# Loading q and k two tokens to a packet in an attention and mixture-of-experts kernel

## The chip, the cores and the metric

The kernel runs on one core of a Trainium2 chip. The metric is the time of one execution on the device in microseconds (us). Before the change it is 764.48 us, the median of three runs (762.65 to 764.74).

A core has five engines that work side by side, each on its own list of instructions in fixed order: TensorE (PE in the profile; its weight loads are a row of their own, PEld), VectorE (DVE), ScalarE (ACT), GpSimd (POOL) and SyncE (SP), which here only issues transfers. They meet at semaphores. Sixteen DMA engines move data between HBM and the on-chip memory SBUF. TensorE writes to a second memory, PSUM, from which VectorE and ScalarE take its results.

## The reference, cut to what matters

```
B, H, S, D = 8, 8, 576, 64                # q, k, v: [B, H, S, D] f32
# attention on tokens averaged four by four (144 of them), repeated four times
out_up    = repeat(softmax(mean4(q) @ mean4(k).T / 8) @ mean4(v), 4)
# attention of each token to the tokens at a distance below 4
out_local = softmax(where(|i - j| < 4, q @ k.T / 8, -1e9)) @ v
x = (out_up + out_local) as [4608 tokens, 512]
# each token goes to one of 8 experts
logits = x @ w_gate + modality_bias[modality_id]
e = argmax(logits); g = softmax(logits)[e]
out = g * (relu(x @ w1[e]) @ w2[e])       # w1: [8, 512, 1024], w2: [8, 1024, 512]
```

## The kernel before

**Units.** Attention goes in 32 units, four to a batch entry; a unit is two heads, one on partitions 0 to 63 and one on 64 to 127 of what TensorE makes. Two units share one load of q and k: `load_qk(b, half)` brings four heads of both into `qt` and `kt`, with 96 tokens on the partitions (token 96 j + p on partition p). `tp` (L253 to L259) transposes 96 tokens of both heads at once, three times into one PSUM tile; `qT` (ScalarE, L271) scales and copies that into 288 columns of `qT`, `kT_` (VectorE, L275) into 288 columns of `kT`. A unit has two such halves (i = 0, 1) for q and two for k. The local scores (`sc`, L304) are 96 small products a unit on a mask that `mk` (L295) puts into PSUM first; the averaged tokens are sums over `qT` and `kT` (`qd`, `d`, `kd`), their scores `scd` (L331). Local probabilities go through a 32x32 transpose (`lt`) and `Pw_` (L372) to `avl` (L408), the product with v; the averaged ones through `pdt` (L378) and `PdT` to `avd` (L393). `X` adds both.

v comes twice: `load_v` as overlapping windows of 32 tokens, 24 apart (`vw`, two buffers by batch entry, a packet of 256 B for each window row and head), and `load_vg` as eight tokens to a packet (`vg`, three buffers) for the averages that GpSimd makes (`vt`, `vd_`).

**Order.** All this is written out by hand. `PHASE` gives each step of a unit a time, in units, after the unit's start; `build` makes a list of (unit + phase, function) in `calls`, sorts it, and calls it in a manual schedule. An engine's instructions stand in that order. Loads are in the same list: `load_qk` of half h at unit time 2 h - 2.02, `load_vg` of unit n at n - 0.14, `load_v` of the next batch entry in four parts from 4 b + 3.65 on. The loads before the loop (both halves of q and k of batch entry 0, v, the gate weights, the modality ids and biases in `Consts.load`) are issued first. `Consts.biases` (L154) turns the modality ids with a product on TensorE (L160) into a table of biases for all tokens; it is called at time 3.05.

**Router.** After four units a batch entry's tokens are routed: logits (`lg`, `LT`, `lgt`, `L`), the argmax and counts on VectorE (`ch1`, `ch2`, 8.39 and 8.55 after the start of the entry's first unit), the place of each token (`pr`, `pl`), a scatter of token numbers by GpSimd (`st`) and the store of the rows (`xr`, `R`, `store`) to HBM.

**Early units.** The experts work in units of 256 tokens of one expert. Two of them (`KEARLY`) are made up from the first five batch entries, before attention ends: `Router.early` counts tokens (a product, L574), makes a table of units (`units_of`, `table`, `index`: some twenty small VectorE instructions) and leaves `eidx` and `eei`; then GpSimd gathers entries and rows (`entries`, `gather`), `Moe.xsplit` transposes the rows on TensorE and splits them into a high part (ScalarE, L777) and the rest (VectorE, L778), and `Moe.wload` and `wsplit` load weights and split them in the same way (L729, L730). `early` is one call at t, just after the last scatter of batch entry 4 (unit time 26.22); each `xsplit` and `wsplit` is one call too.

After attention, `compute` and `second` run the experts' products (L794, L841) for all units, fed by weights that SyncE loads and ScalarE and VectorE split; the late table is made by `Router.late` with the same helpers.

Of the kernel before, what the change touches and what calls it, by code (L numbers as in the profile page):

```python
# [24 lines left out]
NB = 6  # L25
# [39 lines left out]
}  # L65

# [106 lines left out]
class Attention:  # L173
# [23 lines left out]
    def load_qk(s, b, half):  # L197
        nc = s.nc

        qt = s.ld.tile([96, 2, 6, 2, D], F32, name="qt")  # L200
        kt = s.ld.tile([96, 2, 6, 2, D], F32, name="kt")
        for g in range(2) if (b, half) == (0, 0) else (slice(0, 2),):
            for t, src in ((qt, s.q), (kt, s.k)):
                for a in range(2):
                    h = src[b, 4 * half + 2 * a : 4 * half + 2 * a + 2]
                    if g in (0, 1):
                        nc.sync.dma_start(t[:, g, :, a], h[g].rearrange("(j p) d -> p j d", j=6))
                    else:
                        nc.sync.dma_start(t[:, :, :, a].rearrange("p g j d -> p (g j) d"),
                                          h.rearrange("g (j p) d -> p (g j) d", j=6))  # L210
        s.QK[2 * b + half] = (qt, kt)

    def load_v(s, b, part):
# [39 lines left out]
    def tp(s, n, nm, i):  # L253

        src = s.QK[n // 2]["qk".index(nm)]
        p = s.t["tp", nm, n, i] = s.ps.tile([128, 3, 96], F32, name="tp", tag="T", bufs=3)
        for j in range(3):
            s.nc.tensor.transpose(p[:, j, :], src[:, n % 2, 3 * i + j].rearrange("p a d -> p (a d)"),
                                  s.C.ident[:96, :96])  # L259
# [7 lines left out]
    def qT(s, n, i):  # L267
# [3 lines left out]
        s.nc.scalar.mul(s.t["qT", n][:, 288 * i : 288 * i + 288], p.rearrange("m j p -> m (j p)"), QS)  # L271

    def kT_(s, n, i):
        p = s.t.pop(("tp", "k", n, i))
        s.nc.vector.tensor_copy(s.kT[n % 2][:, PAD + 288 * i : PAD + 288 * i + 288], p.rearrange("m j p -> m (j p)"))  # L275
# [149 lines left out]
class Router:  # L425
# [145 lines left out]
    def counts(s, nm):  # L571
        nc = s.nc
        cp = s.ps.tile([128, NE], F32, name="cp", tag="A", bufs=2)
        nc.tensor.matmul(cp, s.C.ones, s.acc, start=True, stop=True)  # L574
        c = s.tp.tile([128, NE], F32, name=nm + "c")
        nc.vector.tensor_copy(c, cp)
        return c

    def units_of(s, c, add, n, nm):

        ni = s.tp.tile([128, NE], I32, name=nm + "ni")
        s.nc.vector.tensor_scalar(ni, c, float(add), None, op0=ALU.add)
        s.nc.vector.tensor_scalar(ni, ni, 8, None, op0=ALU.logical_shift_right)
        s.nc.vector.tensor_copy(n, ni)

    def table(s, n, base, U, nm, pool, tag):
# [6 lines left out]
        nc.vector.tensor_tensor(m, C.ltri[:, :N, :N], n.unsqueeze(1).broadcast_to([128, N, N]), op=ALU.mult)  # L593
        nc.vector.tensor_reduce(incl, m, op=ALU.add, axis=AX.X)
        excl = tp.tile([128, N], F32, name=nm + "excl")
        nc.vector.tensor_tensor(excl, incl, n, op=ALU.subtract)

        off = tp.tile([128, N], F32, name=nm + "off")
        nc.vector.scalar_tensor_tensor(off, excl, -float(UNIT), base, op0=ALU.mult, op1=ALU.add)
        sh = [128, U, N]  # L600
# [6 lines left out]
        nc.vector.tensor_tensor(oh, incl.unsqueeze(1).broadcast_to(sh), ub, op=ALU.is_gt)  # L607
        nc.vector.tensor_tensor(o2, excl.unsqueeze(1).broadcast_to(sh), ub, op=ALU.is_gt)
        nc.vector.tensor_tensor(oh, oh, o2, op=ALU.subtract)
        r = tp.tile([128, 2, U], F32, name=nm + "r")  # L610
        for i, qv in enumerate((off, C.e2[:, :N])):
            nc.vector.tensor_tensor(o2, oh, qv.unsqueeze(1).broadcast_to(sh), op=ALU.mult)
            nc.vector.tensor_reduce(r[:, i], o2, op=ALU.add, axis=AX.X)
        nc.vector.scalar_tensor_tensor(r[:, 0], C.uf[:, :U], float(UNIT), r[:, 0], op0=ALU.mult, op1=ALU.add)
        return r, incl, excl

    def index(s, r, U, nm, count=None):
# [5 lines left out]
                                op=ALU.add)  # L623
        ei = tp.tile([128, U + 1], I32, name=nm + "ei")
        nc.vector.tensor_copy(ei[:, :U], r[:, 1, :U])
        if count is not None:
            nc.vector.tensor_copy(ei[:, U : U + 1], count)
        return idx, ei

    def early(s, K):  # L630
# [6 lines left out]
        nc.vector.tensor_scalar(d, excl, -1.0, float(K), op0=ALU.mult, op1=ALU.add)  # L637
        nc.vector.tensor_scalar(d, d, 0.0, None, op0=ALU.max)
        nc.vector.tensor_tensor(d, d, n, op=ALU.min)
        return s.index(r, K, "e")  # L640

    def late(s, c, pool):
# [4 lines left out]
        s.units_of(c, UNIT // 2 - 1, n[:, :NE], "m")  # L647
        s.units_of(c, UNIT - 1, n[:, NE:], "mh")
# [5 lines left out]
        s.r, s.incl, _ = s.table(n, base, NUMAX, "m", pool, "o")  # L654
        return s.index(s.r, NFULL + 1, "m")

    def rest(s):
# [13 lines left out]
        return s.index(r, NLOOP, "r", cnt)  # L671


class Moe:
# [25 lines left out]
    def chunk(s, e, which, c):  # L700
        return s.wsplit(s.wload(e, which, c), which)
# [12 lines left out]
    def wsplit(s, raw, which):  # L714
        nc = s.nc
        i = s.cw % s.nw
        s.cw += 1
# [7 lines left out]
        with ExitStack() as order:  # L725
            if HOLD <= s.cw <= NHOLD and s.after:
                for x in s.after:
                    order.enter_context(s.tc.issue_after(x.ins))
            nc.scalar.copy(hi, raw)  # L729
            nc.vector.tensor_tensor(lo, raw, hi.bitcast(F32), op=ALU.subtract)  # L730
# [355 lines left out]
```

## Time and profile before

| | |
|---|---|
| median of three runs | 764.48 us |
| profiled execution: its time, its span | 764.05 us, 762.4 us |
| TensorE busy, of it in 380 to 762.4 us | 695.0 us, 373.47 us |
| VectorE, ScalarE, GpSimd busy | 472.6, 422.2, 321.7 us |
| DMA packets, of them under 512 B | 207335, 134941 |
| granted TensorE clock, mean | 0.95 |

The span runs from the first to the last instruction of the program; the rest of the execution's time lies around it. A busy row counts the union of an engine's instructions; TensorE's ends are modelled, so back-to-back products count as busy throughout. A wait is put down to whatever released the semaphore last; "issue" means that nothing in the profile released it. "L258" is a line of the kernel, "tp<-ident,qt" what is written and read, "96*128" rows and columns of the array that are used, "x3" that three like it follow each other. The attention units run from about 6 to 311 us, the experts' products from about 296 us to the end.

### The profile page before, as it was taken

Reading aid. Unit: us, or ns where it says so; the run is one execution under the profiler, and the core shown is the slowest. Engines: PE = TensorE matmul, PEld = TensorE weight load, DVE = VectorE, ACT = ScalarE, POOL = GpSimd, SP = SyncE. Lnnn points to the kernel's source line nnn. Section 1 sums busy time; section 2 is a strip of 40 time slices with the busy share of each in tenths; the row PEclk is TensorE's granted clock in tenths of the full one; section 3 lists DMA queues with packets and bytes.
Section 4 is the critical chain, followed back from the end, with each engine's and each line's share of the span. In section 5 each row is a group of like instructions: output and inputs, shape, how many; then the busy total and the mean of one; then the engine's idle time right before and its main releaser. Section 6 shows DMA issues by size and latency. Waiting matters only on the chain. (4 is left out here: it accounts for less than half of the span.)

```text
span 762.4 us, 20954 instructions
## 1 busy us (share of the span) xinstructions
PE 695.0 (91%) x8307; PEld 599.1 (79%) x8307; DVE 472.6 (62%) x956; ACT 422.2 (55%) x876; POOL 321.7 (42%) x369
## 2 busy tenths in 40 slices
PE   7499888999888978997899999999999999999995
PEld 4387666777666757885898899988999888999894
DVE  4377856778586867784765556555566555565620
ACT  2267756676655676754565545555546455465620
POOL 5365839486776867034433323223232242222101
PEclk8589998999997999998899999999999999999998
DMA  9999999989987982749797666766676766666500
GB/s 180 162 172 193 161 194 178 216 167 196 201 163 163 192 221 99 214 147 302 264 317 240 208 230 227 242 223 215 205 269 208 236 210 213 226 221 228 188 13 19
DMA packets 207335, 151.00 MB, mean 198 GB/s; under 512 B 134941, under 2 KB 173889, under 8 KB 207234
## 3 DMA queue, kind: packets, MB, share of 16 engines
q1 hardware_dynamic: 198978, 130.41, 68.4%
q0 software_dynamic: 8256, 19.22, 7.2%
q8 instruction: 67, 1.10, 0.7%
q14 instruction: 34, 0.28, 0.1%
HBM read 130.38 MB, written 19.47 MB: 197 GB/s over the span
## 5 line engine op out<-in xcount | busy, mean ns | idle before, releaser
L730 DVE TENSOR_TENSOR wlo<-raw,whi 128x1024 fp32r<-128x1024 f32 x130 | 159.3, 1235 | 135.8 <-ACT whi L729 134.9
L729 ACT CAST whi<-raw 128x1024 fp32r<-128x1024 f32 x130 | 135.5, 1048 | 126.7 <-PE l L794 60.2
L794 PE MATMUL l<-xh,wlo 128*128 128x256 f32 x488 | 139.1, 285 | 0.0
L794 PE MATMUL l<-xh,whi 128*128 128x256 f32 x488 | 138.3, 285 | 0.7 <-ACT xh L777 0.7
L794 PE MATMUL l<-xl,whi 128*128 128x256 f32 x488 | 138.7, 285 | 0.0
L845 POOL DMA_INDIRECT out_dram<-o,tg x37 | 42.0, 1134 | 172.2 <-ACT o L844 135.5
L841 PE MATMUL l<-whi,hl 128*128 128x512 f32 x256 | 100.5, 393 | 0.0
L841 PE MATMUL l<-wlo,hh 128*128 128x512 f32 x256 | 100.4, 393 | 0.0
L841 PE MATMUL l<-whi,hh 128*128 128x512 f32 x256 | 98.3, 397 | 0.0
L794 PEld LDWEIGHTS l<-xh,whi 128*128 128x128 f32 x488 | 93.4, 192 | 1.9 <-ACT xh L777 1.1
L794 PEld LDWEIGHTS l<-xl,whi 128*128 128x128 f32 x488 | 93.1, 191 | 1.0 <-issue 0.5
L794 PEld LDWEIGHTS l<-xh,wlo 128*128 128x128 f32 x488 | 93.3, 191 | 0.3 <-issue 0.2
L743 POOL DMA_INDIRECT tg<-tab,midx x33 | 38.7, 1173 | 76.8 <-DMA out_dram<-o,tg 71.1
L797 DVE SCALAR_TENSOR_TENSOR hl<-l,hh 128x512 fp32r<-128x512 f32 x72 | 49.3, 685 | 23.9 <-ACT hh L796 23.9
L753 POOL DMA_INDIRECT xg<-xs,tg x37 | 40.1, 1083 | 51.1 <-DMA tg<-tab,midx 40.8
L372 ACT COPY Pw<-lt 32x288 f32<-32x288 f32 x128 | 55.0, 430 | 9.5 <-DVE lt L367 7.8
L796 ACT ACTIVATE hh<-l 128x512 fp32r<-128x512 f32 x72 | 42.8, 594 | 29.5 <-PE l L794 29.4
L841 PEld LDWEIGHTS l<-wlo,hh 128*128 128x128 f32 x256 | 48.1, 188 | 10.8
L841 PEld LDWEIGHTS l<-whi,hl 128*128 128x128 f32 x256 | 48.1, 188 | 10.6 <-issue 0.5
L841 PEld LDWEIGHTS l<-whi,hh 128*128 128x128 f32 x256 | 48.1, 188 | 10.2
L408 PE MATMUL avl<-Pw,vw 128*64 128x96 f32 x768 | 44.2, 267 | 10.5 <-ACT Od L398 4.6
L564 POOL DMA_INDIRECT tab<-ig,si x36 | 36.8, 1023 | 38.0 <-DVE mn L649 26.6
(203 smaller groups left out, 1398.6 us busy)
## 6 DMA issues: line engine op xcount, KB each, us to landing
raw<-in_moe_w_dram SPq DMA_DIRECT2D x152, 512.0 KB
vw<-in_v_dram SPq DMA_DIRECT2D x124, 96.0 KB
vg<-in_v_dram SPq DMA_DIRECT2D x32, 288.0 KB
xs<-R SPq DMA_DIRECT2D x36, 256.0 KB
qt<-in_q_dram SPq DMA_DIRECT2D x30, 288.0 KB
kt<-in_k_dram SPq DMA_DIRECT2D x30, 288.0 KB
xg<-xs,tg POOLq DMA_INDIRECT x37
out_dram<-o,tg POOLq DMA_INDIRECT x37
```

Of the source, the lines that this page charges most:

```text
L372: s.nc.scalar.copy(s.Pw[n % NPW][r, :, j, :SUB], s.t["lt", n][r, :, :SUB])
L408: s.nc.tensor.matmul(p[64 * a : 64 * a + 64, c], vw[:, NB * (4 * (hp // 2) + hp % 2 + 2 * a) + k, :], Pw[:, NB * a + k], start=True, stop= ...
L564: i = nc.gpsimd.indirect_dma_start(out=s.tab[:, :], out_offset=bass.IndirectOffsetOnAxis(ap=C.si[:, t : t + 1], axis=0), in_=C.ig[:, t, :] ...
L729: nc.scalar.copy(hi, raw)
L730: nc.vector.tensor_tensor(lo, raw, hi.bitcast(F32), op=ALU.subtract)
L743: nc.gpsimd.indirect_dma_start(out=T[:, h, :], out_offset=None, in_=s.tab[:, :], in_offset=bass.IndirectOffsetOnAxis(ap=idx[:, u, h : h + ...
L753: s.gathered = nc.gpsimd.indirect_dma_start(out=R[:, h, :], out_offset=None, in_=s.xs[:n, :], in_offset=bass.IndirectOffsetOnAxis(ap=T[:, ...
L794: nc.tensor.matmul(p[:, f, :], a[:, k, fs], x[:, k, :], start=(k == 0 and i == 0), stop=(k == 3 and i == 2))
L796: nc.scalar.activation(hh[:, 2 * c : 2 * c + 2, :], p, AF.Relu)
L797: nc.vector.scalar_tensor_tensor(hl[:, 2 * c : 2 * c + 2, :], p, 0.0, hh[:, 2 * c : 2 * c + 2, :].bitcast(F32), op0=ALU.max, op1=ALU.subtract)
L841: nc.tensor.matmul(p, a[:, f, hs], x[:, f % 2, :], start=(f == 0 and i == 0), stop=(f == 7 and i == 2))
L845: nc.gpsimd.indirect_dma_start(out=s.out[:, :], out_offset=bass.IndirectOffsetOnAxis(ap=T[:, h, 0:1], axis=0), in_=o, in_offset=None, boun ...
```

## The change

`load_qk` puts tokens 2 x and 2 x + 1 into one packet (512 B), x = 96 c + p on partition p, and brings a half of q, and one of k, in one transfer each in place of two (the very first half stays in pieces by head). Since the two heads of a unit no longer stand side by side in SBUF, `tp` no longer transposes: for each head it multiplies 96 tokens with the identity into its 64 partitions, six products for three transposes. `qT` and `kT_` write every second column.

`load_v` takes its width: 12 windows a transfer as before at the start, 24 in the loop, so 8 transfers a batch entry in place of 16. At the start, vg of unit 0 and v of heads 0 to 3 are queued ahead of the second half of q and k. `biases` moves from unit time 3.05 to 5.05.

`early` becomes a generator with a pause after each instruction; 26 calls, 0.07 of a unit apart, step through it from 24.65 on (its index now ahead of the three instructions for `d`). `xsplit` and `wsplit` are stepped through likewise, in seven calls 0.15 or 0.1 apart and in two calls 0.25 apart. In the late table and the loops nothing changes: `whole` runs a generator to its end.

```diff
 def load_qk(s, b, half):
-        qt = s.ld.tile([96, 2, 6, 2, D], F32, name="qt")
-        for g in range(2) if (b, half) == (0, 0) else (slice(0, 2),):
-            for t, src in ((qt, s.q), (kt, s.k)):
-                for a in range(2):
-                    h = src[b, 4 * half + 2 * a : 4 * half + 2 * a + 2]
-                    if g in (0, 1):
-                        nc.sync.dma_start(t[:, g, :, a], h[g].rearrange("(j p) d -> p j d", j=6))
-                    else:
-                        nc.sync.dma_start(t[:, :, :, a].rearrange("p g j d -> p (g j) d"),
-                                          h.rearrange("g (j p) d -> p (g j) d", j=6))
+        qt = s.ld.tile([96, 2, 2, 3, 2, D], F32, name="qt")
+        for g in range(2) if (b, half) == (0, 0) else (None,):
+            for t, src in ((qt, s.q), (kt, s.k)):
+                h = src[b, 4 * half : 4 * half + 4]
+                if g is None:
+                    nc.sync.dma_start(t.rearrange("p a g c t d -> p (a g c) (t d)"),
+                                      h.rearrange("h (c p t) d -> p (h c) (t d)", p=96, t=2))
+                else:
+                    for a in range(2):
+                        nc.sync.dma_start(t[:, a, g].rearrange("p c t d -> p c (t d)"),
+                                          h[2 * a + g].rearrange("(c p t) d -> p c (t d)", p=96, t=2))
 def load_v(s, b, part, W=4):
-            n0, n1 = NB * 2 * part, NB * 2 * part + NB * 2
+            n0, n1 = NB * part, NB * part + NB * W
 def tp(s, n, nm, i):
-        for j in range(3):
-            s.nc.tensor.transpose(p[:, j, :], src[:, n % 2, 3 * i + j].rearrange("p a d -> p (a d)"),
-                                  s.C.ident[:96, :96])
+        for c in range(3):
+            for a in range(2):
+                s.nc.tensor.matmul(p[64 * a : 64 * a + 64, c, :], src[:, a, n % 2, c, i], s.C.ident[:96, :96],
+                                   start=True, stop=True, skip_group_check=True)
 def qT(s, n, i):
-        s.nc.scalar.mul(s.t["qT", n][:, 288 * i : 288 * i + 288], p.rearrange("m j p -> m (j p)"), QS)
+        s.nc.scalar.mul(s.t["qT", n].rearrange("m (x t) -> m x t", t=2)[:, :, i], p.rearrange("m c p -> m (c p)"), QS)
 def kT_(s, n, i):
-        s.nc.vector.tensor_copy(s.kT[n % 2][:, PAD + 288 * i : PAD + 288 * i + 288], p.rearrange("m j p -> m (j p)"))
+        T = s.kT[n % 2][:, PAD : PAD + S].rearrange("m (x t) -> m x t", t=2)
+        s.nc.vector.tensor_copy(T[:, :, i], p.rearrange("m c p -> m (c p)"))
...
 def early(s, K):
-        s.units_of(s.counts("e"), 0, n, "e")
-        r, _, excl = s.table(n, s.C.ecap, K, "e", None, None)
+        yield from s.units_of((yield from s.counts("e")), 0, n, "e")
+        r, _, excl = yield from s.table(n, s.C.ecap, K, "e", None, None)
+        s.found = yield from s.index(r, K, "e")
...
 def build(...):
             at.load_qk(0, 0)
+            at.load_vg(0)
+            at.load_v(0, 0, 2)
+            at.load_v(0, 2, 2)
             at.load_qk(0, 1)
-            at.load_vg(0)
-            for j in range(4):
-                at.load_v(0, j)
             at.load_vg(1)
+            at.load_v(0, 4, 2)
+            at.load_v(0, 6, 2)
             at.load_vg(2)
...
-                    for j in range(4):
-                        call(4 * b - 1 + used + 0.3 + 0.4 * j, at.load_v, b + 1, j)
+                    for j in range(2):
+                        call(4 * b - 1 + used + 0.3 + 0.8 * j, at.load_v, b + 1, 4 * j)
...
-            call(3.05, C.biases, tc, cp, work, ro.wk, ps)
+            call(5.05, C.biases, tc, cp, work, ro.wk, ps)
...
-            call(t, first)
+            for i in range(26):
+                call(min(t, 4 * (EB - 1) + P["ch2"] + 0.1) + 0.07 * i, first)
...
-            call(t + 4.2, split, 0)
+            for j in range(7):
+                call(t + 4.2 + 0.15 * j, split, 0)
...
-                call(t + 5 + 0.6 * c, wsplit, c)
+                for j in range(2):
+                    call(t + 5 + 0.6 * c + 0.25 * j, wsplit, c)
```

More of the change, by code (lines that the diff above doesn't have):

```diff
@@ L65, with whole @@
 }
+def whole(pieces):
+    while True:
+        try:
+            next(pieces)
+        except StopIteration as x:
+            return x.value
 class Consts:
@@ L729, in wsplit @@
             nc.scalar.copy(hi, raw)
+        yield
+        with ExitStack() as order:
+            if HOLD <= turn <= NHOLD and s.after:
+                for x in s.after:
+                    order.enter_context(s.tc.issue_after(x.ins))
             nc.vector.tensor_tensor(lo, raw, hi.bitcast(F32), op=ALU.subtract)
@@ L1013, in split @@
             if i < len(order):
-                Xs[i] = early[i][3] if i < KEARLY else moe.xsplit(Rs[i], order[i][2])
+                Xs[i] = early[i][3] if i < KEARLY else whole(moe.xsplit(Rs[i], order[i][2]))
         def step():
```

69 lines of the change are left out of this document (51 added, 18 removed).

## The prediction

> **What bounds the kernel now.** I read the page first. Its chain of waits ends after 4 us, at the loop at the end of the program, so it says nothing of the 750 us before.
>
> ```profile
> span 762.4 us, 20954 instructions
> PEclk8589998999997999998899999999999999999998
> DMA  9999999989987982749797666766676766666500
> q8 instruction: 67, 1.10, 0.7%
> ```
>
> So I cut the span at the places where the work changes and read the busy times by stretch (columns: stretch, its length, busy us and count of PE, PEld, DVE, ACT, POOL, then granted clock, DMA share, GB/s).
>
> ```profile
> 21.20:30.60 9.40, 0.00 (x0) 0.00 (x0) 0.22 (x1) 0.00 (x0) 3.17 (x5) 0.50 0.80 151
> 67.00:222.00 155.00, 136.25 (x3074) 108.30 (x3072) 114.50 (x350) 102.81 (x323) 103.49 (x130) 0.94 1.01 187
> 222.00:247.30 25.30, 19.11 (x354) 15.05 (x353) 17.46 (x51) 11.98 (x37) 17.55 (x21) 0.80 0.79 160
> 380.00:762.40 382.40, 373.47 (x2399) 339.23 (x2397) 205.78 (x215) 193.94 (x249) 99.60 (x87) 0.99 0.63 207
> ```
>
> The experts' half (from 380) is TensorE without holes; the change has nothing there. Attention (to about 300) has TensorE at 88% (136.25 of 155), VectorE at 74%, the DMA engines always with something queued (share 1.01). Two stretches stand out: 9.4 us in which TensorE does nothing, and 25.3 us in which it gets through few products. The waits of TensorE, for 0 to 40 us (first row) and for 40 to 300 (the others: in total, times, longest), say who is to blame:
>
> ```profile
> PE mp L160 <- DVE mf L158: 9.4, 1, 9.4
> ...
> PE sc L295 <- DVE le L317: 7.3, 7, 5.4
> PE xr L546 <- issue: 4.2, 1, 4.2
> PE avl L408 <- issue: 3.1, 1, 3.1
> PE pr L520 <- DVE oh L500: 3.0, 5, 1.3
> PE tp L258 <- DMA kt<-in_k_dram: 1.2, 1, 1.2
> ```
>
> Full queues are not late data: after 40 us a q or k transfer holds TensorE for 1.2 us in all. What costs is one wait of 9.4, one of 5.4, and waits ended by nothing that the profile shows ("issue").
>
> **The change, part by part.**
>
> *Start: biases later, v before the second half of q and k.* The rows of SyncE and TensorE at the start:
>
> ```profile
> 7.26 2.88 SPq L209 DMA_DIRECT2D kt<-in_k_dram  x2
> 26.24 0.36 SPq L113 DMA_DIRECT2D R<-in_moe_modality_id_dram  x1
> 29.50 1.97 SPq L209 DMA_DIRECT2D kt<-in_k_dram  x2
> 14.88 0.71 PE L258 MATMUL tp<-ident,kt 96*128 96x96 f32 x3 [2.67 <-DMA kt<-in_k_dram]
> 20.50 0.69 PE L258 MATMUL tp<-ident,kt 96*128 96x96 f32 x3
> 30.63 0.29 PE L160 MATMUL mp<-ident,mf 36*128 36x36 f32 x1 [9.44 <-DVE mf L158]
> 39.73 0.74 PE L258 MATMUL tp<-ident,qt 96*128 96x96 f32 x3
> 40.27 0.69 PE L258 MATMUL tp<-ident,kt 96*128 96x96 f32 x3
> ```
>
> The modality ids are queued at 26.24 behind all first loads; `biases`, called at unit time 3.05, transposes them, and in TensorE's fixed order all of units 0 to 3 stands behind it. At 5.05 its data are long there, so that wait goes. Next late are k of units 2 and 3 (used at 14.88) and the q and k of unit 4 (used at 39.73 and 40.27). Ahead of the first now stand one vg of 288 KB and the v of four heads (767 KB by the shapes in the code), 1.08 MB; what moves at which rate:
>
> ```profile
> 8.60:13.20 4.60, 2.48 (x110) 2.12 (x110) 2.62 (x10) 0.87 (x3) 2.85 (x10) 1.00 1.39 201
> 15.60:23.40 7.80, 5.59 (x122) 4.57 (x122) 3.36 (x12) 1.91 (x8) 4.68 (x6) 0.50 1.31 185
> 380.00:400.00 20.00, 20.00 (x129) 18.16 (x128) 13.94 (x14) 13.52 (x16) 6.77 (x6) 1.00 0.93 320
> ```
>
> In the first of these stretches only q and k move (256 B packets, 201 GB/s), in the second v (185), in the third expert weights in packets of 1 and 2 KB (320). The moved 1.08 MB cost 5.8 us at 185. A half of q and k is 1.18 MB, 5.9 us at 201. Packets of 512 B are not in this trace; their rate lies between 201 and 320, so a half takes 5.9 to 3.7 us. One doubling from 256 B and one from 1 KB, I take the middle of the two by ratio, 254 GB/s: 4.7 us, 1.2 saved a half (0 to 2.2). Two halves stand before that k: 14.88 + 5.8 - 2.4 = 18.3. From there TensorE needed 6.3 us to the end of the 20.50 row (21.19), so it is at the old stall's end at 24.6 instead of 30.63: **6.0 us earlier** (3.6 if packets save nothing, 8.0 if 2.2 a half). The q and k of unit 4: their k was issued by 31.47; three halves cheaper that is 27.9, and at the first use data were taken 4.7 us after the issue ended (10.14 to 14.88), so 32.6, before the 34.3 (40.27 - 6.0) at which they are wanted. Without any saving 36.2 against 36.7: still no wait. The clock stays at half through this stretch in my sum, as it is from 21.2 on.
>
> *q and k later on, one transfer a half, v in 8 transfers for 16.* Over the fifteen remaining halves this takes about 18 us off the queue, and some issue time from SyncE, but the 1.2 us row bounds what TensorE can get: 0 taken, cover being the prefetch. If the cover went, a half would still be quicker than now.
>
> *The product in place of the transpose.* Three transposes of 96x128 become six products of 96x64, 128 times: 384 more products and weight loads. The nearest row for the new form is L408, the same tile and columns in f32:
>
> ```profile
> 120.13 0.47 PE L258 MATMUL tp<-ident,qt 96*128 96x96 f32 x3
> 120.44 0.41 PE L258 MATMUL tp<-ident,kt 96*128 96x96 f32 x3
> 120.69 0.60 PE L546 MATMUL xr<-ident,X 128*128 128x128 f32 x4
> ...
> 122.10 0.72 PE L408 MATMUL avl<-Pw,vw 128*64 128x96 f32 x12
> ```
>
> Three transposes hold TensorE from start to start for 0.31 and 0.25 us, 0.28. Twelve half-wide products end after 0.72; the last alone lasts 0.27 (next fence), so starts are 0.041 apart, six take 0.25: two halves run side by side. Times 128 that is -4 us; with 0.72/12 = 0.06 for each, +10. I take 0, since starts are what the next one waits for.
>
> The Trainium skill, TensorE: Matmul & The Clock Gate, Terms, gives fp32 a transpose mode four times as fast as a product, and TensorEngine Tiling (Array Packing), Restrictions, says column tiling excludes it. By that the six products would take some four times their pass; the f32 product L408 shows no such price against the transposes, so the sum goes by the row.
>
> *Strided copies.* kT and qT are written to every second column. Rows by form:
>
> ```profile
> L408 PE MATMUL avl<-Pw,vw 128*64 128x96 f32 x768 | 44.2, 267 | 10.5 <-ACT Od L398 4.6 <-issue 3.1 <-ACT Pw L372 2.6
> L275 DVE COPY kT<-tp 128x288 f32<-128x288 f32 x64 | 28.2, 440 | 15.5 <-PE tp L258 15.2
> L271 ACT ACTIVATE qT<-tp 128x288 f32<-128x288 f32 x64 | 26.0, 406 | 38.1 <-PE tp L258 38.0
> L372 ACT COPY Pw<-lt 32x288 f32<-32x288 f32 x128 | 55.0, 430 | 9.5 <-DVE lt L367 7.8
> ```
>
> L372 writes 24 of 32-wide runs and takes 430 against 406 ns. At worst +24 ns in 128 copies, 3 us spread over two engines with a quarter of their time free: 0 taken, 0 to 3.
>
> *The early table in pieces.* Now it is one run on VectorE:
>
> ```profile
> 224.75 1.90 DVE L582 TENSOR_SCALAR eni<-ec 128x8 int32<-128x8 f32 x1
> ...
> 231.75 0.16 DVE L625 CAST eei<-er 128x2 int32<-128x2 f32 x1
> 232.23 0.32 PE L295 MATMUL sc<-mask,identb 128*128 128x192 bf16 x1 [5.38 <-DVE le L317]
> 231.70:242.00 10.30, 9.77 (x159) 7.81 (x159) 7.39 (x24) 5.53 (x17) 5.53 (x8) 0.50 0.89 198
> ```
>
> 7.2 us without a score subtraction between; TensorE stands 5.4 us, and after it the clock is halved for 10.3 us. Its whole price: 354 matmuls in 222.0 to 247.3 at the 155/3074 us of the stretch before are 17.8 us, so 7.5 of the 25.3 are lost. In pieces 0.07 apart, 26 calls spread over 1.8 units, some 15.7 us at 8.6 a unit (155 us for 18 units); VectorE has 26% of that free, 4.1 us, for 7.2 of work. Up to 3.1 come back as delay; fewer if the 1.90 is not repeated. I take 1.5: **6.0 gained** (4.4 to 7.5). Behind the pieces POOL's first entries wait for less. A new wait: the counts product now follows `ch2` at once, in TensorE's order ahead of its next transposes; the `pr` row has that same dependence, 3.0 in five, 1.3 at most. **-0.5** (0 to -1.3).
>
> *Splits in pieces.* VectorE no longer stands in its order behind ScalarE's copy:
>
> ```profile
> DVE xl L778 <- ACT xh L777: 3.6, 1, 3.6
> ```
>
> That is the largest of these in 245 to 300; TensorE has little of it. **1.0** (-1 to 3).
>
> *Instructions.* 768 more for TensorE. "Issue" waits of 4.2 and 3.1 are fetches, I think: 16,614 PE and PEld instructions by 67 packets of q8 is one packet per 248, and q8 has no packet from 88 to 95 us, one from 95 to 97.5:
>
> ```profile
> q8 instruction: 1, 0.02, 3.5%
> ```
>
> and TensorE resumes at 98.39. Three packets more, against emptier queues: 0 taken, from -7.3 (both waits go) to +7.3 (both double).
>
> The Trainium skill, Runtime: NRT & Kernel Launch, Instruction fetch mechanics, has the fetch of 256 instructions mostly hidden. By it the fetches of rival 2 could neither come nor go; the 4.2 us row speaks against it.
>
> **Sum.** 6.0 + 6.0 - 0.5 + 1.0 = 12.5 us. The profiled execution took 764.05 us (span 762.4 and 1.65 around it), the median is 764.48: no difference. 764.05 - 12.5 = **751.5**.
>
> **Rivals.**
> 1. *The stall only moves.* The first 67 us are bound by transfers as a whole; unit 4, or unit 8's k (the 1.2 us row), then stands where the ids stood. For it: the DMA share above 1 all that time. Against: three halves are cheaper and the sum left 1.7 us. Only table and splits remain: 757.5.
> 2. *Fetches come later.* 512 B packets in bigger transfers put more bytes ahead of a fetch: 751.5 + 7.3 = 758.8. Or *both waits vanish*: 744.2.
> 3. *Slower: the two halves of a product pair do not overlap.* Then six products take 6 x 0.093 = 0.56 for 0.28, 128 times: 36 us, of which attention's 12% of free TensorE time (19 in 155) hides perhaps 10. 751.5 + 26 = 778. It decides from 0.38 us a group on (12.5/128 over 0.28). Against it: the avl row of 122.10.
>    The fp32 rule of the Trainium skill named above would show in this way.
> 4. *The pieces do not help*, VectorE being as long in sum: 757.5.
>
> **How the numbers follow.** Forecast 0.63, rival 1 0.12, later fetches 0.07, vanished fetches 0.06, rival 3 0.06, rival 4 0.06. About 0.3%, 2.3 us, is what can be told from no change. Rival 3 and a bad meeting of 1 and 2 give slower 0.08; those and 1 with 4 near no change, 0.07; faster 0.85. The forecast's own bounds, 3.6 + 4.4 - 1.3 - 1 = 5.7 to 8.0 + 7.5 + 3 = 18.5, give 746 to 758; fetches and strided copies widen that to 742 to 762.
>
> **What would show it.** No wait of L160 above 1 us, and unit 4's first tp near 33.7; a wait of unit 2's tp for k until about 18. No idle TensorE around the table and a full clock there. Groups of six tp products near 0.25 us start to start. PE's issue waits near 7 us. kT and qT copies at 440 and 406 ns. Wrong if tp products are 0.06 apart or more, if a DMA holds unit 4 to 8 by several us, or if fetch waits pass 12 us.

## The result and the profile after

The changed kernel takes 816.53 us (median of four executions, 810.24 to 824.9), the kernel before 763.82 beside it: a ratio of **1.0636, 95% interval 1.0583 to 1.069**. That is 53 us slower by the medians and 49 by the ratio, where 13 us faster was forecast. An execution over 1.5% longer than the fastest of its kernel is left out of the ratios here and below, but not of the medians, and the profiles of e3, e9 and e13 are of such executions. All the profiles below are of single executions; the changed kernel's took 810.24 us.

The page of the changed kernel, four rows that answer to those shown of before:

```profile
span 808.6 us, 23175 instructions
...
PEclk8778989799899899899989999999999999999998
DMA  9998598859797895356689766766666666666600
...
q8 instruction: 76, 1.25, 0.8%
```

2221 instructions more and nine packets more on q8, a queue of instructions, where the prediction counted 768 and three. The DMA engines, nearly full through most of attention before, now have holes; and after 40 us no wait of TensorE names a load of q or k.

Where the time went: the last product of attention in the timeline of TensorE, before (first fence) and after (second).

```profile
309.69 1.21 PE L408 MATMUL avl<-Pw,vw 128*64 128x96 f32 x24
```

```profile
355.02 0.72 PE L420 MATMUL avl<-Pw,vw 128*64 128x96 f32 x12
```

The first row holds the last two groups of twelve, the second the last one alone. By their ends, 310.90 and 355.74, attention ends 44.8 us later, of 46.2 that the span is longer. The experts' half is within 1.4 us of what it was; nearly all of it happened in attention. TensorE's groups by form, before and after (busy us in the first 312 or 360 us, mean ns of one record):

```profile
L258 PE MATMUL tp<-ident,qt 96*128 96x96 f32 x192 | 32.0, 280 | 2.5 <-issue 1.6 <-DMA qt<-in_q_dram 0.9
L258 PE MATMUL tp<-ident,kt 96*128 96x96 f32 x192 | 29.6, 267 | 5.3 <-DMA kt<-in_k_dram 4.5 <-issue 0.8
```

```profile
L269 PE MATMUL tp<-ident,kt 96*64 96x96 f32 x768 | 51.5, 273 | 12.0 <-issue 8.4 <-DMA kt<-in_k_dram 3.4
L269 PE MATMUL tp<-ident,qt 96*64 96x96 f32 x768 | 49.9, 269 | 9.0 <-DMA qt<-in_q_dram 7.1 <-DVE kT L287 1.2 <-issue 0.7
```

32.0 + 29.6 became 49.9 + 51.5: 39.8 us more. And the count says why: 64 groups of six products are 384 for q and as many for k, and the profile has 768 records of each. **One f32 product is two records**, each with a weight load of its own. Two groups follow each other in the timeline of TensorE after:

```profile
45.33 0.67 PE L269 MATMUL tp<-ident,qt 96*64 96x96 f32 x12
45.83 0.67 PE L269 MATMUL tp<-ident,kt 96*64 96x96 f32 x12
46.42 0.25 PE L169 MATMUL mp<-ident,mf 36*128 36x36 f32 x1
```

0.50 and 0.59 us from start to start, for 0.31 and 0.25 of three transposes. (Over the trace a group of products takes 0.50 to 0.65 us and one of transposes 0.25 to 0.34, by what follows it.) The second thing that is larger is TensorE's waits that nothing in the profile ends, from 40 to 300 us (in total, times, longest):

```profile
PE sc L316 <- issue: 13.1, 8, 3.5
PE tp L269 <- issue: 5.9, 3, 4.6
PE avl L420 <- issue: 5.0, 2, 3.9
PE scd L343 <- issue: 3.2, 2, 2.1
PE sc L307 <- DVE le L329: 2.1, 1, 2.1
```

With a row of 0.5 that is not shown these are 27.7 us of "issue", where such rows of before make 11.2. A second profile of the kernel before (e0 below) has 21.8, so a single profile does not tell how much of this is the change's. What these waits are the trace shows: of 13 above 1 us from 40 us to the end of attention, 12 end 1.2 to 1.8 us after a packet of 16 KB of the instruction queue has landed. They are waits for instructions. The two stalls that were to go did go: there is no wait of L169 above 1 us, and le's longest is 2.1 us where it was 5.4. The first row of tp in units 2, 4 and 8 after, with k's for units 2 and 4 (the rows between are left out):

```profile
17.59 1.23 PE L269 MATMUL tp<-ident,qt 96*64 96x96 f32 x12 [5.95 <-DMA qt<-in_q_dram]
20.40 1.23 PE L269 MATMUL tp<-ident,kt 96*64 96x96 f32 x12 [1.58 <-DMA kt<-in_k_dram]
33.69 0.72 PE L269 MATMUL tp<-ident,qt 96*64 96x96 f32 x12 [1.16 <-DMA qt<-in_q_dram]
36.26 1.23 PE L269 MATMUL tp<-ident,kt 96*64 96x96 f32 x12 [1.85 <-DMA kt<-in_k_dram]
78.36 0.72 PE L269 MATMUL tp<-ident,qt 96*64 96x96 f32 x12
```

Unit 4 begins at 33.69, the time that was forecast and 6.0 us earlier than in the profile of before; unit 8 begins at 78.36, 11.4 us later than there (67.0). What the start gained was gone four units on. How much was gained is uncertain: in seven other profiles with the old start unit 4 begins between 35.8 and 38.9 us, not at 39.7.

### The profile page after: what moved, and what is told of

Its sections match the earlier page's. It is cut to its first block, busy times and chain, and to the rows that moved or that the text cites. A ratio compares the mean times of both kernels' runs of the same rounds, so it can differ in the third digit from the quotient of the medians.

```text
span 808.6 us, 23175 instructions
## 1 busy us (share of the span) xinstructions
PE 738.5 (91%) x9459; PEld 643.2 (80%) x9459; DVE 474.9 (59%) x956; ACT 425.4 (53%) x876; POOL 322.7 (40%) x369
## 5 line engine op out<-in xcount | busy, mean ns | idle before, releaser
L282 ACT ACTIVATE qT<-tp 128x288 f32<-128x288 f32 x64 | 27.7, 433 | 92.1 <-PE tp L269 92.1
L297 POOL TENSOR_TENSOR d<-kT 128x288 f32<-128x288 f32 x32 | 21.4, 668 | 110.0 <-DVE kT L287 109.8
L791 POOL DMA_INDIRECT xg<-xs,tg x37 | 42.6, 1150 | 54.6 <-DMA tg<-tab,midx 36.7
L269 PE MATMUL tp<-ident,kt 96*64 96x96 f32 x768 | 51.5, 273 | 12.0 <-issue 8.4
L269 PE MATMUL tp<-ident,qt 96*64 96x96 f32 x768 | 49.9, 269 | 9.0 <-DMA qt<-in_q_dram 7.1
```

The costliest lines, as they stand in the source:

```text
L269: s.nc.tensor.matmul(p[64 * a : 64 * a + 64, c, :], src[:, a, n % 2, c, i], s.C.ident[:96, :96], start=True, stop=True, skip_group_check=True)
L282: s.nc.scalar.mul(s.t["qT", n].rearrange("m (x t) -> m x t", t=2)[:, :, i], p.rearrange("m c p -> m (c p)"), QS)
L791: s.gathered = nc.gpsimd.indirect_dma_start(out=R[:, h, :], out_offset=None, in_=s.xs[:n, :], in_offset=bass.IndirectOffsetOnAxis(ap=T[:, ...
```

## The experiments

The kernel before took 764 us in the first runs and 772 to 774 beside the experiments; each ratio is to the runs of before made with it. One per cent is 7.7 us.

| run | q, k packets, transfer | group in TensorE | start | pieces | ratio (95%) |
|---|---|---|---|---|---|
| the change | 512 B, 576 KB | 6 products | new | yes | 1.0636 (1.0583 to 1.069) |
| e15 | 512 B, 144 KB | 6 products | new | yes | 1.0374 (1.027 to 1.0479) |
| e2 | 512 B, 576 KB | 3 transposes | new | yes | 1.0202 (1.0134 to 1.0271) |
| e6 | 256 B, 576 KB | 3 transposes | new | yes | 1.0112 (1.0029 to 1.0194) |
| e5 | 512 B, 144 KB | 3 transposes | new | yes | 1.0066 (1.0019 to 1.0113) |
| e1 | 256 B, 288 KB | 3 transposes | new | yes | 1.0047 (1.0011 to 1.0084) |
| e7 | as before | as before | new | no | 1.0036 (0.9999 to 1.0073) |
| e14 | as before | as before | new, later v as before | no | 0.9991 (0.9954 to 1.0028) |
| e10, e17 | as before | as before | biases only | no | 0.9947 (0.9915 to 0.998), 0.9985 (0.9948 to 1.0021) |
| e8 | as before | as before | as before | yes | 0.9976 (0.9932 to 1.002) |
| e11 | as before | as before | biases only | yes | 1.0034 (0.9997 to 1.0071) |
| e16 | 256 B, 144 KB | as before | biases only | no | **0.9926 (0.9888 to 0.9964)** |
| e3 | as before | 6 products | as before | no | 1.0352 (1.0284 to 1.0419) |
| e4 | as before | 3 transposes twice | as before | no | 1.0057 (1.0008 to 1.0106) |
| e9 | as before | 9 small matmuls more | as before | no | 1.0578 (1.0508 to 1.0648) |
| e12 | as before, less v | as before | as before | no | 0.9894 (0.9826 to 0.9963) |
| e13 | as before, less v | 6 products | as before | no | 1.0291 (1.0226 to 1.0355) |

### The products: e3, e4, e9, e12, e13

**e3**, the kernel before with the products and nothing else:

```
-        for j in range(3):
-            s.nc.tensor.transpose(p[:, j, :], src[:, n % 2, 3 * i + j].rearrange("p a d -> p (a d)"), ident[:96, :96])
+        for j in range(3):
+            for a in range(2):
+                s.nc.tensor.matmul(p[64 * a : 64 * a + 64, j, :], src[:, n % 2, 3 * i + j, a], ident[:96, :96], ...)
```

> The kernel before with one thing changed: six products with the identity for three transposes, in the old layout and with the old transfers and copies. Theory: + 0.27 us a group at full clock, twice that while the clock is at half, for 128 groups, is + 35 to 40, and issue waits + 15 to 20 for 2304 more instructions on TensorE: 810 to 822. If the product costs its TensorE time alone and the waits were the transfers': 795 to 802. Rival (the products are hidden in TensorE's free time and the loss is the transfers'): 764 to 775.

1.0352, **27 us**: below what was expected (810 to 822), and near to the case in which the product costs its time on TensorE alone. The waits for instructions came all the same:

```profile
PE sc L305 <- issue: 16.1, 10, 6.3
PE avl L409 <- issue: 7.8, 5, 2.8
```

**e4** does the three transposes twice (`for _ in range(2):` around them).

> The kernel before with each group's three transposes done twice into the same place: TensorE time per group rises from 0.28 to about 0.56 us as with the products, but by 768 instructions on TensorE in place of 2304. Theory (time and instruction fetch both count): 35 us of TensorE time with 5 to 7 us of issue waits, 798 to 808, and 8 to 15 below the products alone. If the fetches don't matter: the same as the products alone within 3 us. If TensorE's free time hides the work: 770 or below.

1.0057, 4.4 us. This was a miss: the group takes nearly as long as the products' group, yet costs a sixth. (On the 764 us from which the expectation reckons, 1.0057 is 768, its third case: TensorE's free time hides the work.) Rows of e4, then of e3:

```profile
121.80 0.71 PE L259 MATMUL tp<-ident,qt 96*128 96x96 f32 x6
122.35 0.66 PE L259 MATMUL tp<-ident,kt 96*128 96x96 f32 x6
122.85 1.13 PE L547 MATMUL xr<-ident,X 128*128 128x128 f32 x4
```

```profile
98.66 0.67 PE L259 MATMUL tp<-ident,qt 96*64 96x96 f32 x12
99.16 0.67 PE L259 MATMUL tp<-ident,kt 96*64 96x96 f32 x12
99.75 0.66 PE L547 MATMUL xr<-ident,X 128*128 128x128 f32 x4
```

0.55 and 0.50, 0.50 and 0.59; by the medians over the trace the products' group is some 0.05 longer. So TensorE time in a group is not by itself the price. Three things differ: e3 has 1536 instructions more, of another form, and e4's granted clock is higher, 0.949 to 0.965 in its nine runs, where the kernel before has 0.931 to 0.95 beside it and e3 0.939 to 0.947. From 40 us to the end of attention e4's profile has a clock of 0.95, and TensorE waits 24.4 us in all (gaps above 0.15 us); e0's has 0.89 and 31.7, e3's 0.91 and 43.5. So e4's longer groups came with fewer waits and a faster clock. That these paid for the second transposes is an inference; no run sets the clock.

**e9** adds as many instructions as the products, without f32 passes or column tiles:

```
+        for x in range(9):
+            s.nc.tensor.matmul(p[:32, 0, :2], s.C.dummy[:, :32], s.C.dummy[:, :2], start=True, stop=True, ...)
```

> The kernel before with nine small bf16 matmuls (32 stationary columns, 2 moving ones, into columns that the transposes then overwrite) ahead of each group of three transposes: 18 more instructions on TensorE a group, 2304 in all, as many as the products add, without their f32 passes or column tiles. The transposes done twice added nearly the products' TensorE time with 768 instructions and cost 0.6%; the products cost 3.5%. Theory (the number of instructions, through their fetch, is the larger part of the products' price): issue waits of TensorE 30 or more, ratio 1.025 to 1.04. Rival (it is something in the products themselves, the f32 passes or the change of tiles): issue waits near 13, ratio 1.005 to 1.015.

1.0578, more than either theory. The small matmuls were not small:

```profile
120.08 0.40 PE L258 MATMUL tp<-dummy 128*32 128x2 bf16 x9
120.41 0.58 PE L261 MATMUL tp<-ident,kt 96*128 96x96 f32 x3
120.83 0.60 PE L549 MATMUL xr<-ident,X 128*128 128x128 f32 x4
```

Here the nine take 0.33 us, and the transposes after them 0.42. Over the trace the nine take 0.31, and the transposes some 0.05 more than in the kernel before: 0.36 a group, 46 us for 128 groups, and 45 were paid, at a lower granted clock (0.910 to 0.914). The run does not tell instructions from time.

**e12 and e13** take loads away from in front of the fetches, without and with the products:

```
         vw = s.vw[b % 2]
+        if b > 1:
+            return
```

> The kernel before with the v windows of batches 2 to 7 not loaded (the windows of the first two batches are used again, so local attention takes wrong values): about 7 MB less on the data queue during attention. It is the partner of the next run. Expected: issue waits of TensorE from 10 to 20 us down to 5 or less, as there is little ahead of a fetch; attention ends 5 to 15 us sooner, ratio 0.980 to 0.995.

> The run with the products alone, with the v windows of batches 2 to 7 not loaded (wrong values, as in the partner run). Against the partner it tells the products' TensorE time from their instruction fetches. If the price of the products (27 us with all loads) is their time on TensorE: again 22 to 30 us above the partner, issue waits or not. If it is mostly fetches that stand behind loads: 12 us or less above the partner, with issue waits back from 35 to about 10.

e12 0.9894 and e13 1.0291: the products cost 0.0397 or **31 us** here too, no less than with all loads. But issue waits of TensorE, from the start to the end of attention, went only from 34.9 (e3) to 26.7 us (e13), and from 21.8 (e0) to 18.0 (e12), where 5 or less was expected: what stands in front of a fetch was not taken away, as the lag of a q or k transfer (from its issue to its last packet, as explained below) stayed (3.6 us in e3, 3.5 in e13), though 9.4 MB less were moved. It speaks for the products' time and leaves the fetches open.

What this group settles: the products are the largest term, 0.031 to 0.043 or **24 to 33 us** in four pairs of runs (e15 to e5, e3 to before, e13 to e12, the change to e2), against 40 us more on TensorE. What stays open is the split between that time, the fetches and the clock.

### The size of a transfer: e2, e5, e6, e15

**e2** is the changed kernel with transposes. Two tokens to a packet leave the two heads of a token apart, so a block of 96x128 holds two tokens of one head:

```
-                s.nc.tensor.matmul(p[64 * a : 64 * a + 64, c, :], src[:, a, n % 2, c, i], ident[:96, :96], ...)
+            s.nc.tensor.transpose(p[:, c, :], src[:, i, n % 2, c].rearrange("p t d -> p (t d)"), ident[:96, :96])
```

> The changed kernel with everything of it, but for the six products of a group three transposes of 96x128 blocks; a block then holds two tokens of one head where two heads of one token belong, so the scores are formed of other rows than the reference's. Transfers, copies and pieces are those of the changed kernel. Theory (products are the loss): 816.5 - 0.27 x 128 = 35, and some 20 us of issue waits go too: 755 to 765, or as low as 750 if the packets help the start. Rival (512 B packets, one transfer a half, or the strided copies hold attention up): stays above 795.

1.0202, 788 us: neither theory. The products are 33 of the 49 us, and 16 are left without them. With no more instructions than before, TensorE's issue waits (40 to 330 us) make 37.9 us, more than the 30.9 of the changed kernel; the longest rows:

```profile
PE sc L314 <- issue: 14.7, 8, 5.7
PE avd L403 <- issue: 8.4, 4, 3.5
PE tp L268 <- issue: 6.5, 3, 4.4
```

One of them shows what it waited for. SyncE issues a half of q and of k at 54.72 and 55.14 (SPq is SyncE's queue); TensorE then stands from 62.02 on:

```profile
54.72 0.32 SPq L215 DMA_DIRECT2D qt<-in_q_dram  x1
55.14 2.20 SPq L215 DMA_DIRECT2D kt<-in_k_dram  x1
...
67.72 0.42 PE L314 MATMUL sc<-kT,qT 64*24 64x32 f32 x16 [5.70 <-issue]
```

The DMA queues of e2 from 57.8 to 64.4 us, and from 64.4 to 66.3 us:

```profile
q1 hardware_dynamic: 2406, 1.35, 111.1%
```

```profile
q1 hardware_dynamic: 363, 0.25, 92.0%
q8 instruction: 1, 0.02, 5.8%
```

Packets of 512 B are q's and k's alone here, and the 2304 of this half start between 56.50 and 66.99. From 57.8 to 64.4 there is no fetch packet; one starts at 64.44, when 2199 of the 2304 have started, has landed at 66.21, and TensorE goes on 1.5 us later. **The fetch came after most of the half of q and k.** That it had been asked for earlier and stood behind them is an inference: the profile does not show when a fetch is asked for.

**e5, e6, e15** separate packet from transfer:

```
# e5 (on e2) and e15 (on the changed kernel): four transfers of one head
-                    nc.sync.dma_start(t.rearrange("p a g c t d -> p (a g c) (t d)"), h.rearrange("h (c p t) d -> p (h c) (t d)", ...))
+                    for a, g: nc.sync.dma_start(t[:, a, g].rearrange("p c t d -> p c (t d)"), h[2 * a + g]...)
# e6 (on e2): one transfer, 256 B
+                    nc.sync.dma_start(t.rearrange("p a g c t d -> p (a g c t) d"), h.rearrange("h (j p) d -> p (h j) d", p=96))
```

> The run with token pairs transposed (its scores are of other rows than the reference's), with one thing changed: a half of q or of k comes in four transfers of one head each (144 KB) in place of one of 576 KB; packets stay at 512 B. That run had 38 us of issue waits of TensorE and took 1.020 of the kernel before, with no more instructions than that. Theory Q (a fetch of instructions stands behind what is queued on the data queue, and what is queued counts in transfers): the lag of a q or k transfer falls from 6 to below 4 us, issue waits to 5 to 15, the ratio to 1.00 to 1.01. Theory P (what is queued counts in packets, and 512 B packets are twice the bytes each): lag and waits stay (30 to 40 us), the ratio 1.015 to 1.025. Rival (fetches aren't behind the loads at all): waits the same and the lag the same.

> The same run with the other half undone: packets of 256 B again, but one transfer of 576 KB a half; blocks of 96x128 of rows in another order are transposed (the scores are of other rows than the reference's). Theory Q (queued transfers count): lag near 6 us or more, issue waits 30 to 40, ratio 1.015 to 1.025. Theory P (queued packets count): lag near 4, issue waits 5 to 15, ratio 1.00 to 1.01.

> The changed kernel complete and right, with one thing other: a half of q or of k comes in four transfers of one head (144 KB) in place of one of 576 KB. If what the size of a transfer cost the run with transposes (1.0202 to 1.0066) is a term of its own in the changed kernel too: 1.0636 - 0.0136 = 1.050, between 1.042 and 1.056, with less issue waits than 31 us. If it is swallowed by the products' longer TensorE time: 1.060 or above.

The lag of a transfer here is the time from the end of its issue to its last packet, the bytes of SyncE's issues matched in order with those of the queue; a mean over all q and k transfers between 33 and 330 us. (Counted by the 512 B packets themselves, from the end of the issue of a half to its last packet, it is 8.4 us in e2 and 4.3 in e5: the same order.)

```
run  packet  transfer   lag    ratio
e5   512 B   144 KB    3.4 us  1.0066
e1   256 B   288 KB    4.0 us  1.0047
e6   256 B   576 KB    5.4 us  1.0112
e2   512 B   576 KB    6.1 us  1.0202
```

e5 falls in line with theory Q in lag and ratio, though its issue waits (23 us) are longer than Q had them; e6 lies between Q and P. In small transfers the packet costs nothing that can be measured (e5, 1.5 us over e1 with its 288 KB); with one transfer a half, e2 is 0.0090 or 7 us above e6, by intervals that overlap, so a cost of the packet there is open. The one transfer a half costs 0.0136, **10 us**, with 512 B. In the changed kernel itself it is 0.0262, 20 us (e15), more than expected; by e15's interval it lies between 12 and 28. There the issue waits fall, as expected, but only from 30.9 to 26.4 us; the granted clock from 40 us to the end of attention goes from 0.89 to 0.92 (in e2 and e5 from 0.86 to 0.89). So the 20 us are not the fetch waits alone, and what else they are is not shown.

### Start and pieces: e1, e7, e14, e10, e17, e8, e11, e16, e0

**e1** is the changed kernel with `load_qk`, `tp`, `qT` and `kT_` of the kernel before.

> The changed kernel with the packets undone: q and k loaded, transposed three to a group and copied as in the kernel before; biases at 5.05, v before the second half, table and splits in pieces stay. Theory (the products are the loss, start and table gain what was forecast): 764 - 6 - 6 - 1 = 751 to 753 us, groups of three transposes 0.28 us start to start, issue waits of TensorE from 40 to 330 us back near 11. Rival A (start or pieces lose by themselves): 764 or above. Rival B (both gain less than forecast): 755 to 761.

1.0047: rival A. Start and pieces together lose 3.6 us where 12.5 were to be gained.

**e7** has the start alone (first loads reordered, v in half as many transfers, biases at 5.05); **e14** the same with the later v as before (`call(..., at.load_v, b + 1, 2 * j, 2)`, four times); **e10** and **e17** one number:

```
-            call(3.05, C.biases, tc, cp, work, ro.wk, ps)
+            call(5.05, C.biases, tc, cp, work, ro.wk, ps)
```

> The kernel before with the first loads reordered, biases at 5.05 and v in half as many transfers; nothing else. The prediction: 6 us less without the packets' 1.2 a half it was 3.6, ratio 0.992 to 0.996. Rival 1 (the stall only moves, unit 4 waits for its q and k): 1.000. From the run without packets, where ScalarE waited 21 us for the rows' stores in place of 3.3: those waits come from the v transfers in halves, and the ratio is 1.002 to 1.010.

> The run with the start alone (1.0036), with the v of later batches again in 16 transfers a batch at the old times; the new order of the first loads and biases at 5.05 stay. If the halved number of v transfers took back the gain of the biases (0.9947): 0.994 to 0.998. If the new order of the first loads did: 1.002 to 1.005.

> The kernel before with one number changed, biases at 5.05 for 3.05; loads in their old order. The wait of 9.4 us for the ids goes; next late are the q and k of unit 4, whose data came about 36 us in where they would be wanted at 31: 4 us less, ratio 0.993 to 0.997. Rival (the start is bound by its transfers, what is gained at unit 4 is lost by unit 8): 0.999 to 1.002.

> The run with the biases alone once more, on the same chip as the one beside it and in more rounds: 0.9947 before, with an interval of 0.9915 to 0.998. If that gain is real: 0.992 to 0.997. If it was the spread of these runs: 0.998 to 1.002.

e7 1.0036, e14 0.9991 (between its two cases), biases 0.9947 and 0.9985: of the forecast 6 us there are 1 to 4 with the biases alone, whose second interval holds 1, and none with the new order. By its expectation e17 says that the gain of e10 was the spread of these runs. **e0**, the kernel before once more, gives the base:

> The kernel before unchanged, for its profile on the chip of these runs: 768 to 778 us where its first profile took 764, with issue waits of TensorE between 12 and 20 us.

It took 771.5 us. Units 4 and 8 in e0, then in e14 (rows of tp that begin a unit, or wait):

```profile
35.94 0.47 PE L258 MATMUL tp<-ident,qt 96*128 96x96 f32 x3
69.12 0.41 PE L258 MATMUL tp<-ident,qt 96*128 96x96 f32 x3
```

```profile
35.12 0.52 PE L258 MATMUL tp<-ident,qt 96*128 96x96 f32 x3 [1.00 <-DMA qt<-in_q_dram]
38.96 0.71 PE L258 MATMUL tp<-ident,kt 96*128 96x96 f32 x3 [3.32 <-DMA kt<-in_k_dram]
69.77 0.41 PE L258 MATMUL tp<-ident,qt 96*128 96x96 f32 x3
```

The wait for the ids (7.8 us in e0) became waits for q and k, 8.8 and 6.9 us in e14 to the end of attention, and unit 8 starts where it did. With the start alone the first 70 us are bound by their transfers: rival 1 of the prediction.

**e8** has the pieces alone, **e11** pieces and biases.

> The kernel before with the early table and the splits in pieces and nothing else. The prediction: 7 us less, ratio 0.990 to 0.993; no wait of sc for le above 2 us near 227, and TensorE at full clock after it. Rival 4 (VectorE is as long in sum, the pieces give back what they save): 1.000, with several waits of 1 to 3 us around it in place of the one of 5.4.

> The kernel before with biases at 5.05 and the table and splits in pieces; loads, transposes and copies as before. This is the part of the change that none of the runs spoke against. If both bring something, 0.990 to 0.996; if the start is bound by transfers, 0.996 to 0.999.

0.9976 and 1.0034: no gain that can be measured, where 7 us were forecast for the pieces; both lie outside the gains that were expected. TensorE's longest wait for le between 205 and 300 us is 4.3 to 6.7 us in ten of the twelve kernels without pieces, 1.6 and 1.9 in the others (e0, e13), and 1.2 in e8 and e11. So the kernel before itself was profiled without the stall, and was no faster for it (e0, 771.5 us). What came in its place is seen in e11, on GpSimd, VectorE and TensorE:

```profile
237.19 0.98 POOL L778 DMA_INDIRECT tg<-tab,eidx  x1 [6.37 <-DMA tab<-ig,si]
...
239.77 1.49 PE L387 MATMUL pdt<-ident,de 128*72 128x128 f32 x6 [3.75 <-POOL de L370]
...
242.14 0.58 DVE L376 STREAM_TRANSPOSE lt<-le 128x384 f32<-128x384 f32 x1 [5.43 <-POOL le L366]
```

GpSimd's first gather of entries stands 6.4 us in GpSimd's order, and with it the two multiplications that VectorE and TensorE need. GpSimd's wait is as long in the kernel before. There it is put down to z of VectorE, but the gather begins 7.7 us after the end of the last scatter's instruction there as here:

```profile
POOL tg L743 <- DVE z L347: 6.4, 1, 6.4
```

There it lay in part under TensorE's own stall (229.8 to 236.1 us, the stall 226.9 to 232.2). With the table in pieces the cover is gone: TensorE waits for `de` 1.3 to 4.7 us in six of the eight kernels with pieces, in none of the twelve without.

**e16**, what the runs point to: biases at 5.05, and the q and k of the kernel before in transfers of one head (`for x in (0, 1): nc.sync.dma_start(t[:, x, :, a], h[x]...)`).

> The kernel before with biases at 5.05 and each transfer of q and k cut in two, one head (144 KB, 256 B packets) in place of two. From 576 to 144 KB the ratio fell by 1.4 to 2.6% with 512 B packets, lag 6.1 to 3.4. If smaller still helps from 288 KB on: lag near 3, ratio 0.988 to 0.993, below the biases alone. If 288 KB was small enough, or SyncE's doubled issues cost as much: 0.994 to 0.999.

0.9926, 766.15 against 773.27 us: **faster than both kernels**, by 0.7% against the kernel before, with a lag of 2.7 us; both as the first case expected. How much of it is the transfers', the interval of e17 beside it leaves open.

## Why the prediction was wrong, point by point

One path from the kernel before to the changed one: start and pieces +3.6 us (e1), 512 B packets in small transfers and strided copies +1.5 (e5), one transfer a half +10.5 (e2), products +33.5 (the change): 49 us or 0.0636 of 772. The prediction had -12.5, 0, 0 and 0. On another path, with the products in before the transfers are made large, the transfers come out at 20 and the products at 24.

- **"Twelve half-wide products end after 0.72 ... so starts are 0.041 apart, six take 0.25": this step failed first.** The row's x12 are the records of six f32 products. Read so, six take some 0.5, as measured (0.50 to 0.59), and the term that was put at nothing measured 24 to 33 us. The prediction's own count of L408, x768 for all units, told it: 32 units with twelve products each are 384. Rival 3, which gave 0.56 a group and +26 us, had the size of it (27 in e3); it had a chance of 0.06. Its reason, that the halves of a pair don't overlap, is not shown: twelve records in 0.50 are 0.042 apart, as the prediction had them, only twice as many. The rule for fp32 of the Trainium skill that stood beside it (TensorE: Matmul & The Clock Gate, Terms) gives a transpose mode four times as fast for fp32; an estimate by it would make 1.1 us of 0.28. The group went to twice.
- **"q and k later on, one transfer a half ...: 0 taken."** 10 to 20 us lost. The prefetch did cover the data, as argued: after 40 us no row of TensorE's waits names a load of q or k in the changed kernel. What shows instead are late fetches of instructions, which the prediction named as rival 2 and priced at +7.3; from e2 to e5 they fall by 15 us. The mechanism was there, its size wrong, and in the changed kernel they are not the whole of the loss (e15). The Trainium skill (Runtime: NRT & Kernel Launch, Instruction fetch mechanics) has the price of a fetch mostly hidden. That does not hold here: the issue waits make 27.7 us in the changed kernel and 11.2 and 21.8 in the two profiles of the kernel before.
- **"Packets: 254 GB/s, 4.7 us a half."** The size was nearly right. In the changed kernel two stretches at the start move hardly anything but 512 B packets:

```profile
14.00:18.00 4.00, 0.41 (x6) 0.44 (x8) 1.94 (x7) 0.00 (x0) 0.53 (x1) 0.65 1.20 237
30.00:34.00 4.00, 2.84 (x128) 2.25 (x126) 2.88 (x10) 3.76 (x13) 3.52 (x6) 1.00 1.07 235
```

At 236 GB/s a half takes 5.0 us, 0.9 less than at the 201 of 256 B packets, where 1.2 was forecast. No gain of it is seen in the time of any run.
- **"6.0 us earlier" at unit 4**: the time was met (33.69 against 33.7) by luck, and not in the way of the sum. k of units 2 and 3 was taken at 20.40 where the sum had 18.3; and unit 4, for which the sum had no wait, stood 1.16 us for its q, and its k was taken at 36.26 where the sum had it ready at 32.6. The 39.73 of before was late for that kernel, too (35.94 in e0). And the sum stopped at unit 4: unit 8 began 11.4 us later than before, and at 78.55 in e2, without the products, too.
- **"Early table: 6.0 gained"**: the stall went, as forecast, and GpSimd's, which had lain in part under it, came out. Nor was the stall a fixed price of the kernel before: in e0 it is 1.6 us. "POOL's first entries wait for less" was the false sentence: they wait 8.1 us in the changed kernel for the scatter of the router's table.
- **Strided copies**: 453 and 433 ns for 440 and 406, as bounded; no effect seen.
- **Instructions**: 768 more were counted; 2304 came on TensorE, by the same misreading (2221 is the balance of all engines).

## What to carry to other kernels

Check a row's count against the loops of the code before dividing its time by it: an f32 product is two records here, a transpose one. When a stall is taken out of an engine, look for waits of the other engines at the same time, as long as it: they may surface. Take a second profile of the kernel before pricing a stall: here one of 5.4 us was 1.6 the second time. And where a program is fetched while it runs, a large transfer can cost time though its own data come early enough; cutting it in four gave back 10 us in one kernel and 20 in the other, part of it as shorter waits for instructions.

## What the runs showed of the hardware that was not expected

- TensorE goes on 1.2 to 1.8 us after a packet of 16 KB of instructions has landed (12 of 13 issue waits above 1 us in the changed kernel). In e2 such a packet started only when 2199 of 2304 packets of a half of q and k, issued from 54.72 us on, had started (the fetch at 64.44).
- Packets of 512 B moved at 235 to 237 GB/s, those of 256 B at 201.
- Three transposes done twice, 0.5 us a group, cost 4.4 us in all, with a granted clock of 0.949 to 0.965 for 0.931 to 0.95; products that take some 0.05 longer a group cost 27. Why is open.
- Nine bf16 matmuls of two columns, with their weight loads, take 0.31 us, and the f32 transposes behind them some 0.05 more than usual (e9).
